# New instruction lists for five engines: the same operations of a gated mix kernel in another written order

## The chip, the core and the metric

The kernel runs on one core of one Trainium2 chip. The metric is the device time of one execution in microseconds (us); a comparison uses the median of several runs. The engines are named as the profile names them: PE is TensorE (PEld its weight loads), DVE is VectorE, ACT is ScalarE, POOL is GpSimd and SP is SyncE, which here issues all data transfers.

## The reference, cut to what matters

```python
L, D, N, F = 2048, 448, 256, 1792           # u: [1, L, D], float32

def _A_ref(u, ...):                          # a long convolution, its kernel made from a diagonal state space
    dt = exp(log_dt); A = -exp(log_A_real) + 1j * A_imag
    C = (C_real + 1j * C_imag) * dt[:, None]
    P = exp((A * dt[:, None])[:, :, None] * arange(L))
    K = 2.0 * einsum("dn,dnl->dl", C, P).real
    y = irfft(rfft(u_t, 2 * L) * rfft(K, 2 * L))[..., :L]
    return y + u * D_skip

def _B_ref(x, w_gate, w_up, w_down):         # a gated linear unit
    return (sigmoid(x @ w_gate) * (x @ w_up)) @ w_down

g = sigmoid((x * gate_w).sum(-1, keepdims=True))
return g * a + (1 - g) * b                   # a, b: the two above, of the same x
```

## The kernel before

The kernel does three kinds of work side by side.

*The linear unit* (tiles of the pools `glu` and `gps`). The rows of x are taken in halves and blocks of 512, the 1792 hidden columns in 14 pieces of 128. `glu_mm` (L1423 to L1428) makes one PSUM tile `gu` of 128x512 from eleven matmuls, in four operations of three or two: values and weights are split into a rounded part (`xs`, `wh`) and a rest (`wl`), so that one product takes several fast matmuls. ACT takes the gate's tanh into `sg` (L1407), DVE multiplies (L1409 or L1412), ACT and DVE split the product into `hh` and `hl`. `glu_down` (L1443 to L1447) multiplies by the down weights `vh`, `vl` into the one PSUM buffer `dn`, with three matmuls, or for some pieces with one plain float32 matmul (L1443), which the profile records as two instructions. DVE adds the result, scaled by one minus the gate, to `ob` (L1462).

*The convolution's kernel* (pools `eg`, `egp`), in 28 chunks of 16 channels. For each, POOL raises powers into `tb`, SP fetches the chunk's phases into `phs`, and `turns` makes angles on PE in two PSUM buffers `tp` (L1232 and L1241), between which ACT rounds (L1236, L1238). ACT then takes sines (L1243, L1244, L1254) into `cs`, DVE multiplies outer products `es` into it (L1261, L1275, L1278), and `contract` (L1290) sums it up on PE, in 32-column quadrants of the array, into `kp`, which ACT copies to `ke` (L1311).

*The transforms* (pools `fu`, `fk`, `fups`, `fkps`), by matmuls with tables: `stage1` (L812) with the table `ft`, of which the pool `fu` holds one buffer of four pieces in turn; a transposition through device memory (`shf`); `spectrum_four` (L845); the product (L889); and the way back (L924). They use row halves, fourths or column halves of the array, and PSUM tiles `fps`.

What sets the order of all this is written out by hand. Each operation has a key: engine, tag of the tile it writes, and a priority number. `PLACE` holds for each key the places of its operations, in the order in which the program makes them, in the list of their engine; each engine, SP with its transfers included, executes its list from front to back. The planner merges the five lists into one sequence and emits it; a tile's buffers are given out in that sequence, and waits follow from who writes and reads each tile.

```python
        for key, places in PLACE.items():
            for o, place in zip(kinds[key], places, strict=True):
                o["place"] = place
        ...
        queue = {e: sorted((o for o in ops if o["eng"] == e), key=lambda o: -o["place"]) for e in engines}
```

Of the kernel before, what the change touches and what calls it, by code (L numbers as in the profile page):

```python
# [28 lines left out]
    ('Act', 'aci', 10): (15, 42,),  # L29
    ('Act', 'aci', 19): (64, 95,),  # L30
    ('Act', 'acr', 10): (14, 40, 53,),
    ('Act', 'acr', 19): (66, 91, 103,),
# [26 lines left out]
    ('Act', 'dots', 1): (28,),  # L59
    ('Act', 'dots', 2): (45,),  # L60
    ('Act', 'dots', 16): (68, 82,),
# [18 lines left out]
    ('Act', 'idn', 10): (13,),  # L80
    ('Act', 'junk', 10): (32, 61,),
    ('Act', 'junk', 19): (78, 81, 143,),
# [12 lines left out]
    ('Act', 'pos_sb', 10): (37, 38,),  # L95
# [25 lines left out]
    ('DVE', 'acr', 19): (152,),  # L121
# [1467 lines left out]
```

## Time and profile before

| | |
|---|---|
| three runs | 687.51, 687.73 and 686.11 us, median 687.51 |
| profiled execution, its own time | 683.66 us |
| its span, first to last instruction | 681.9 us |
| granted TensorE clock, mean | 0.998 |
| PE busy | 669.5 us, 98% of the span, 6568 instructions |
| weight loads (PEld) | 482.7 us, 71% |
| DVE / ACT / POOL busy | 601.7 / 510.3 / 272.4 us (88%, 75%, 40%) |
| data moved | 122.80 MB in 96900 packets, 180 GB/s on the mean |

Matmuls are pipelined in the array and drawn until their results have left it, so that two that follow each other overlap in the profile and the busy time of PE counts time in which nothing new could start; distances between starts tell what a matmul takes. In a line of the waits, the engine, line and tile that waited stand first, then who ended the wait, the total in us, how often, and the longest. In a line of a timeline, the start and the duration in us come first, and in brackets at the end the idle time before the instruction and what ended it. Groups give the total busy time and the mean in ns after the bar, then the idle time before them.

### The profile page before, as it was taken

Reading aid. Unit: us, or ns where it says so; the run is one execution under the profiler, and the core shown is the slowest. Engines: PE = TensorE matmul, PEld = TensorE weight load, DVE = VectorE, ACT = ScalarE, POOL = GpSimd, SP = SyncE. Lnnn points to the kernel's source line nnn. Section 1 sums busy time; section 2 is a strip of 40 time slices with the busy share of each in tenths; the row PEclk is TensorE's granted clock in tenths of the full one; section 3 lists DMA queues with packets and bytes.
Section 4 is the critical chain, followed back from the end, with each engine's and each line's share of the span. In section 5 each row is a group of like instructions: output and inputs, shape, how many; then the busy total and the mean of one; then the engine's idle time right before and its main releaser. Section 6 shows DMA issues by size and latency. Waiting matters only on the chain.

```text
span 681.9 us, 16255 instructions
## 1 busy us (share of the span) xinstructions
PE 669.5 (98%) x6568; PEld 482.7 (71%) x6568; DVE 601.7 (88%) x699; ACT 510.3 (75%) x928; POOL 272.4 (40%) x280
## 2 busy tenths in 40 slices
PE   8999999999999999999999999999999999999996
PEld 7777666877886687676646676788888766556874
DVE  7999999999999999999999999989974389677976
ACT  6688799799999999999999999999842452342110
POOL 0305596554458574494956668534000000000000
PEclk9999999999999999999999999999999999999999
DMA  8969333574893888927977884342969982889855
GB/s 259 247 149 235 100 102 90 132 197 143 225 188 87 178 203 211 262 107 175 183 220 186 180 221 120 123 144 106 208 122 243 278 294 79 269 273 244 148 150 122
DMA packets 96900, 122.80 MB, mean 180 GB/s; under 512 B 31033, under 2 KB 80505, under 8 KB 95801
## 3 DMA queue, kind: packets, MB, share of 16 engines
q1 hardware_dynamic: 96824, 121.76, 69.8%
q8 instruction: 52, 0.85, 0.6%
q14 instruction: 24, 0.19, 0.1%
HBM read 78.16 MB, written 43.58 MB: 179 GB/s over the span
## 4 chain that ended last, share of the span: by engine, by line
PE 73%; ACT 11%; DMA 7%; DVE 5%; issue 2%; SPq 1%; ACTq 0%; DVEq 0%
PE gu_gps L1423 9%; PE gu_gps L1424 8%; PE gu_gps L1425 8%; PE dn_gps L1443 7%; PE kp_egp L1290 6%; PE dn_gps L1445 4%; PE fps_fups L812 4%; PE dn_gps L1446 3%; PE dn_gps L1447 3%; PE tp_egp L1232 3%; PE gu_gps L1427 3%; PE gu_gps L1428 3%; PE tp_egp L1241 3%; DMA us<-fx_fu 3%; DMA ft_fu<-in_s1t_dram 2%; PE fps_fups L889 2%
## 5 line engine op out<-in xcount | busy, mean ns | idle before, releaser
L1423 PE MATMUL gu_gps<-xs_glu,wh_glu 128*128 128x512 f32 x336 | 145.8, 434 | 1.3 <-DVE sg_glu L1412 0.8
L1424 PE MATMUL gu_gps<-xs_glu,wh_glu 128*128 128x512 f32 x336 | 132.0, 393 | 0.0
L1425 PE MATMUL gu_gps<-xs_glu,wl_glu 128*128 128x512 f32 x336 | 131.8, 392 | 0.0
L1278 DVE TENSOR_TENSOR cs_eg<-cs_eg,es_eg 128x2048 f32<-128x2048 f32 x56 | 130.1, 2323 | 1.3
L1222 POOL TENSOR_TENSOR tb_eg<-tb_eg 128x96 f32<-128x96 f32 (+2 forms) x84 | 114.4, 1364 | 6.1
L1261 DVE TENSOR_TENSOR es_eg<-tb_eg 128x1024 f32<-128x1024 f32 x112 | 111.5, 1016 | 2.5
L1423 PEld LDWEIGHTS gu_gps<-xs_glu,wh_glu 128*128 128x128 f32 x336 | 63.3, 189 | 30.3 <-issue 13.5
L1225 POOL TENSOR_TENSOR tb_eg<-tb_eg,bs_eg 128x32 f32<-128x32 f32 x84 | 77.5, 923 | 6.3
L1275 DVE TENSOR_TENSOR cs_eg<-cs_eg,es_eg 128x1024 f32<-128x1024 f32 x56 | 70.5, 1259 | 8.8 <-ACT cs_eg L1254 7.2
L1238 ACT ACTIVATE nn_eg<-cs_eg 128x512 fp32r<-128x512 f32 x112 | 73.1, 653 | 3.8 <-PE tp_egp L1241 2.6
L1424 PEld LDWEIGHTS gu_gps<-xs_glu,wh_glu 128*128 128x128 f32 x336 | 63.3, 188 | 16.4 <-issue 5.6
L1425 PEld LDWEIGHTS gu_gps<-xs_glu,wl_glu 128*128 128x128 f32 x336 | 63.1, 188 | 14.3
L1236 ACT ACTIVATE cs_eg<-tp_egp 128x512 f32<-128x512 f32 x112 | 68.8, 619 | 3.6 <-PE kp_egp L1290 2.2
L1407 ACT ACTIVATE sg_glu<-gu_gps 128x512 f32<-128x512 f32 x56 | 34.1, 609 | 48.8 <-PE gu_gps L1428 47.3
L1243 ACT ACTIVATE cs_eg<-tp_egp 128x512 f32<-128x512 f32 x112 | 67.5, 616 | 2.7 <-PE tp_egp L1241 2.3
L1244 ACT ACTIVATE cs_eg<-tp_egp 128x512 f32<-128x512 f32 x112 | 68.3, 614 | 0.2
L1254 ACT ACTIVATE cs_eg<-cs_eg,half_pi 128x1024 f32<-128x1024 f32 x56 | 66.0, 1179 | 0.1
L1462 DVE SCALAR_TENSOR_TENSOR ob_glu<-dn_gps,og,ob_glu 128x448 f32<-128x448 f32 x70 | 47.4, 677 | 18.4 <-PE dn_gps L1447 17.3
L1290 PEld LDWEIGHTS kp_egp<-cs_eg 128*32 128x32 f32 x3584 | 51.3, 110 | 10.8 <-issue 7.2
L1290 PE MATMUL kp_egp<-cs_eg 128*32 128x64 f32 x3584 | 55.8, 220 | 0.1
L1212 POOL MEMSET tb_eg<- 128x96 f32 x28 | 7.9, 284 | 115.8 <-DVE es_eg L1261 113.6
L1232 PE MATMUL tp_egp<-pos_sb,phs 97*128 97x512 f32 x112 | 50.3, 458 | 1.2 <-ACT cs_eg L1244 1.2
(169 smaller groups left out, 1320.9 us busy)
## 6 DMA issues: line engine op xcount, KB each, us to landing
shf<-fx_fu SPq DMA_DIRECT2D x16, 896.0 KB
fx_fu<-shf SPq DMA_DIRECT2D x16, 896.0 KB
us<-fx_fu SPq DMA_DIRECT2D x16, 896.0 KB
xr_glu<-in_w_dram SPq DMA_DIRECT2D x46, 256.0 KB
uax_fk<-us SPq DMA_DIRECT2D x16, 448.0 KB
ua_fk<-us SPq DMA_DIRECT2D x16, 448.0 KB
xr_glu<-in_w_dram SPq DMA_DIRECT2D x17, 224.0 KB
gt_pre<-in_u_dram SPq DMA_DIRECT2D x8, 448.0 KB
```

Source lines behind the costliest of these rows:

```text
L1222: pool(96 * m, lambda n=n, m=m: G.tensor_mul(g3(n + 1, m), g3(1, m), g3(n, 1).to_broadcast([128, 32, 3, m])))
L1225: pool(32, lambda e=e: G.tensor_mul(t(e + 1), t(e), b(3)))
L1232: op("PE", c_mm(532), lambda: T.matmul(tp.real, phs[:, ph, 128 * nh:128 * nh + 128].bitcast(F32R), pos[:, 512 * i:512 * i + 512], start=Tr ...
L1236: op("Act", c_act(512, True), lambda: S.activation(cs[:, 1, ds, 32:96], block(tp), AF.Copy, bias=MAGIC), [tp], [(cs, ("s", i))], prio)
L1238: op("Act", c_act(512), lambda: S.activation(block(nn), cs[:, 1, ds, 32:96], AF.Copy, scale=-1.0, bias=MAGIC), [(cs, ("s", i))], [nn], prio)
L1261: V.tensor_mul(o.rearrange("p d (i k) -> p d i k", k=ny), x.unsqueeze(3).to_broadcast([128, 16, nx, ny]), y.unsqueeze(2).to_broadcast([128 ...
L1275: op("DVE", c_dve(1024), lambda: V.tensor_mul(cs[:, :, :, 0:32], cs[:, ::-1, :, 63:31:-1], es[:, :, 0:32].unsqueeze(1).to_broadcast([128, ...
L1278: op("DVE", c_dve(2048), lambda: V.tensor_mul(cs[:, :, :, 32:96], cs[:, :, :, 32:96], es[:, :, 32:96].unsqueeze(1).to_broadcast([128, 2, 1 ...
L1290: T.matmul(kp[32 * j:32 * j + 32, q], cs[:, z, 4 * j + q, 64:96], cs[:, z, 4 * j + q, 0:64], start=cs is parts[0] and z == 0 and q == 0, s ...
L1423: T.matmul(p.real, wh[:, k, cs], x[:, k], start=(k == 0), stop=False)
L1424: T.matmul(p.real, wh[:, k, cs], x[:, 4 + k], start=False, stop=False)
L1425: T.matmul(p.real, wl[:, k, cs], x[:, k], start=False, stop=False)
```

## The change

`PLACE` is replaced: for every key the places are numbers found by a new search, "for the best average over three sets of longer durations, fetches and transfers". Nothing else is changed: the same operations with the same operands, sizes and buffers. Of PE's 1043 operations 647 stand at another place, of ACT's 911 578, of DVE's 675 356, of POOL's 276 39 and of SP's 369 transfers 273. The mean distance is 1.43 places on PE, 1.44 on ACT, 1.09 on DVE, 0.24 on POOL and 2.01 on SP, the greatest 12, 23, 24, 8 and 22.

```diff
-    ('Act', 'acr', 10): (14, 40, 53,),
-    ('Act', 'acr', 19): (66, 91, 103,),
+    ('Act', 'acr', 10): (13, 37, 50,),
+    ('Act', 'acr', 19): (63, 91, 103,),
...
-    ('DVE', 'ones', 10): (0,),
+    ('DVE', 'ones', 10): (2,),
...
-    ('DVE', 'rt', 10): (34, 35, 39, 45, 49, 60, 66,),
+    ('DVE', 'rt', 10): (33, 34, 37, 47, 49, 58, 64,),
...
-    ('SP', 'ft', 30): (91, 103, 107, 111, 116, 159, 166, 173,),
+    ('SP', 'ft', 30): (91, 102, 108, 110, 116, 158, 165, 173,),
...
-    ('SP', 'phs', 20): (63, 67, 70, 81, 93, 106, 112, 121, 127, 130, 137, 136, 143, 153, 170, 172, 176, 185, 190, 189,
-        202, 207, 216, 218, 229, 236, 238, 246,),
+    ('SP', 'phs', 20): (60, 67, 74, 80, 103, 107, 112, 121, 125, 130, 137, 136, 148, 163, 167, 174, 175, 184, 189,
+        188, 206, 209, 215, 217, 226, 235, 241, 242,),
...
```

Places of the operations that the prediction speaks of (key, and which of the key's operations, counted from 0). An operation whose own place stays is moved in time by those that now stand before it and no longer do.

| engine | key, number | place before | place after |
|---|---|---|---|
| PE | `fps` 30, 1 and 2 (`stage1`, 141 and 147 us in the profile) | 210, 220 | 212, 220 |
| PE | `gu` 60, 122, 123 and 125 | 214, 218, 211 | 209, 210, 211 |
| PE | `dn` 60, 50 | 208 | 214 |
| PE | `fps` 30, 3 and 4 (155 and 160 us) | 232, 239 | 231, 239 |
| PE | `fps` 30, 19 and 20 (282 and 289 us) | 440, 450 | 440, 451 |
| ACT, PE | `cs` 20, 236 and its reader `tp` 20, 136 (339 us) | 530, 530 | 529, 529 |
| DVE | `ones` 10, 0; `skip` 20, 0; `half_pi` 0, 0 | 0, 1, 25 | 2, 0, 1 |
| DVE, PE | `sg` 5, 2 and the reuse of its PSUM buffer by `gu` 60, 108 (118 us) | 176, 171 | 176, 171 |
| DVE, PE | `rt` 10, 1 and its reader `fps` 10, 0 (17 us) | 35, 14 | 34, 13 |
| SP, PE | `vh` 21, 1 and its reader `dn` 60, 89 (270 us) | 149, 423 | 149, 427 |
| DVE | `ob` 45, 31 (663 us); `ob` 40, 0; `ob` 41, 0 | 650, 649, 646 | 648, 650, 649 |
| DVE, PE | `cs` 20, 79 and its reader `kp` 20, 19 (386 us); `wl` 45, 1 on DVE | 411, 605, 414 | 412, 606, 410 |
| ACT, PE | `cs` 20, 257 and the reuse by `tp` 20, 150 (362 us) | 569, 563 | 569, 563 |
| DVE, PE | `cs` 20, 63 and its reader `kp` 20, 15 (333 us) | 370, 523 | 371, 522 |
| SP | `phs` 20, 13 | 153 | 163 |

More of the change, by code (lines that the diff above doesn't have):

```diff
@@ L28 @@
 PLACE = {
-    ('Act', 'aci', 10): (15, 42,),
-    ('Act', 'aci', 19): (64, 95,),
-    ('Act', 'acr', 10): (14, 40, 53,),
-    ('Act', 'acr', 19): (66, 91, 103,),
[26 rows of a table removed]
-    ('Act', 'dots', 1): (28,),
-    ('Act', 'dots', 2): (45,),
-    ('Act', 'dots', 16): (68, 82,),
[18 rows of a table removed]
-    ('Act', 'idn', 10): (13,),
-    ('Act', 'junk', 10): (32, 61,),
-    ('Act', 'junk', 19): (78, 81, 143,),
[12 rows of a table removed]
-    ('Act', 'pos_sb', 10): (37, 38,),
[13 rows of a table removed]
+    ('Act', 'aci', 10): (15, 40,),
+    ('Act', 'aci', 19): (65, 94,),
+    ('Act', 'acr', 10): (13, 37, 50,),
+    ('Act', 'acr', 19): (63, 91, 103,),
[26 rows of a table added]
+    ('Act', 'dots', 1): (27,),
+    ('Act', 'dots', 2): (47,),
+    ('Act', 'dots', 16): (67, 82,),
[18 rows of a table added]
+    ('Act', 'idn', 10): (12,),
+    ('Act', 'junk', 10): (33, 60,),
+    ('Act', 'junk', 19): (77, 81, 135,),
[12 rows of a table added]
+    ('Act', 'pos_sb', 10): (51, 57,),
[13 rows of a table added]
     ('Act', 'wh', 0): (1, 4,),
     ('Act', 'wh', 1): (6, 7,),
[4 rows of a table removed]
[4 rows of a table added]
     ('Act', 'xs', 0): (0, 2, 3, 5,),
[2 rows of a table removed]
[2 rows of a table added]
     ('DVE', 'aci', 10): (41,),
@@ L120 @@
     ('DVE', 'acr', 10): (89,),
-    ('DVE', 'acr', 19): (152,),
[1 row of a table removed]
+    ('DVE', 'acr', 19): (151,),
[1 row of a table added]
     ('DVE', 'ai', 19): (143,),
[3 rows of a table removed]
[3 rows of a table added]
     ('DVE', 'ci', 19): (140,),
[1 row of a table removed]
[1 row of a table added]
     ('DVE', 'cr', 19): (138, 141,),
[6 rows of a table removed]
[6 rows of a table added]
     ('DVE', 'dt2', 10): (28,),
     ('DVE', 'dtp', 10): (29,),
-    ('DVE', 'dtv', 10): (27,),
[14 rows of a table removed]
-    ('DVE', 'half_pi', 0): (25,),
[24 rows of a table removed]
-    ('DVE', 'ones', 10): (0,),
-    ('DVE', 'p', 10): (16, 17, 19, 21, 22, 23, 26,),
-    ('DVE', 'phs', 20): (2,),
[6 rows of a table removed]
-    ('DVE', 'skip', 20): (1,),
[6 rows of a table removed]
-    ('DVE', 'uax', 40): (536, 539, 546, 547, 561, 558, 571, 572, 575, 579, 584, 585, 591, 590, 596, 595, 622, 623,
[26 rows of a table removed]
+    ('DVE', 'dtv', 10): (26,),
[14 rows of a table added]
+    ('DVE', 'half_pi', 0): (1,),
[24 rows of a table added]
+    ('DVE', 'ones', 10): (2,),
+    ('DVE', 'p', 10): (16, 17, 18, 19, 20, 22, 24,),
+    ('DVE', 'phs', 20): (3,),
[6 rows of a table added]
+    ('DVE', 'skip', 20): (0,),
[6 rows of a table added]
+    ('DVE', 'uax', 40): (536, 538, 545, 546, 556, 561, 571, 569, 575, 578, 583, 582, 591, 590, 595, 596, 622, 623,
[26 rows of a table added]
         1032, 1036, 1040,),
     ('PE', 'fps', -1): (0,),
[6 rows of a table removed]
[6 rows of a table added]
         1039,),
[2 rows of a table removed]
[2 rows of a table added]
         1041,),
[33 rows of a table removed]
[33 rows of a table added]
     ('Pool', 'bsx1', 10): (5, 11,),
     ('Pool', 'bsx1', 19): (17, 49,),
[2 rows of a table removed]
[2 rows of a table added]
         56, 57, 58, 59, 60, 61, 62, 63, 64, 65, 66, 67, 68, 69, 70, 71, 72, 73, 74, 75, 76, 77, 78, 79, 80, 81, 82,
```

510 rows, old and new, of the table PLACE are left out of this document.

## The prediction

> **What bounds the kernel now.** I read the page's first two parts, then the table by windows, then the waits of PE alone, then single gaps in the timeline, and last the grouped lines.
>
> ```profile
> PE 669.5 (98%) x6568; PEld 482.7 (71%) x6568; DVE 601.7 (88%) x699; ACT 510.3 (75%) x928; POOL 272.4 (40%) x280
> ...
> PEclk9999999999999999999999999999999999999999
> ```
> ```profile
> 0.00:50.00 50.00, 48.06 (x195) 36.54 (x196) 43.93 (x102) 34.91 (x61) 6.66 (x11) 1.00 0.84 219
> 50.00:100.00 50.00, 49.42 (x190) 34.56 (x188) 47.52 (x78) 41.90 (x75) 33.47 (x30) 1.00 0.56 150
> 100.00:150.00 50.00, 48.53 (x571) 37.68 (x569) 49.63 (x55) 43.53 (x75) 30.06 (x31) 1.00 0.56 145
> 150.00:200.00 50.00, 49.71 (x602) 39.39 (x591) 48.11 (x45) 48.05 (x89) 26.88 (x30) 1.00 0.70 176
> 200.00:250.00 50.00, 50.00 (x626) 35.87 (x627) 48.56 (x46) 49.84 (x95) 32.73 (x32) 1.00 0.67 148
> 250.00:300.00 50.00, 48.55 (x688) 35.65 (x677) 47.98 (x45) 47.49 (x86) 30.45 (x32) 1.00 0.80 206
> 300.00:350.00 50.00, 48.77 (x667) 32.25 (x666) 48.49 (x47) 48.40 (x88) 36.33 (x37) 1.00 0.79 172
> 350.00:400.00 50.00, 49.93 (x580) 31.98 (x578) 46.63 (x38) 49.76 (x95) 30.25 (x32) 1.00 0.85 213
> ...
> 500.00:550.00 50.00, 50.00 (x379) 39.30 (x378) 22.73 (x34) 18.07 (x34) 0.00 (x0) 1.00 0.88 235
> ...
> 650.00:682.00 32.00, 26.57 (x165) 18.48 (x161) 22.43 (x46) 2.46 (x4) 0.00 (x0) 0.96 0.56 141
> ```
> The columns are length, then busy time of PE, PEld, DVE, ACT and POOL, clock, DMA. PE (TensorE) is busy in 669.5 of 681.9 us, so the end is set by PE's work and by what it loses waiting. Between 100 and 400 us ACT and DVE are nearly full as well (49.84 and 48.56 of 50 in one window), so an operation put too early on PE meets a producer that can't hurry. After 500 us they are under half busy and PE has no idle time. The last 5.4 us are DVE's last additions and the stores. The clock is full until PE has finished.
>
> ```profile
> PE fps_fups L812 <- DMA ft_fu<-in_s1t_dram: 1.8, 4, 0.6
> PE tp_egp L1232 <- ACT cs_eg L1244: 1.2, 1, 1.2
> PE fps_fups L1039 <- DVE ones_pro L1034: 1.1, 1, 1.1
> PE gu_gps L1423 <- DVE sg_glu L1412: 0.8, 1, 0.8
> PE fps_fups L1081 <- DVE rt_pro L1078: 0.6, 1, 0.6
> PE dn_gps L1443 <- DMA vh_glu<-in_w_dram: 0.5, 1, 0.5
> PE tp_egp L1241 <- ACT nn_eg L1238: 0.4, 1, 0.4
> PE gu_gps L1423 <- DVE hh_glu L1409: 0.3, 1, 0.3
> PE dn_gps L1445 <- DVE ob_glu L1462: 0.2, 1, 0.2
> ```
> These twelve waits (total, times, longest) are 6.9 us. That is less than PE loses, since a matmul is drawn longer than its share of the array:
>
> ```profile
> 78.59 0.39 PE L1424 MATMUL gu_gps<-xs_glu,wh_glu 128*128 128x512 f32 x1
> 78.82 0.39 PE L1425 MATMUL gu_gps<-xs_glu,wl_glu 128*128 128x512 f32 x1
> 79.64 0.51 PE L1241 MATMUL tp_egp<-nn_eg,idn 128*128 128x512 f32 x1 [0.44 <-ACT nn_eg L1238]
> 80.13 0.50 PE L1423 MATMUL gu_gps<-xs_glu,wh_glu 128*128 128x512 f32 x1
> 80.46 0.40 PE L1424 MATMUL gu_gps<-xs_glu,wh_glu 128*128 128x512 f32 x1
> ```
> Undisturbed starts are 0.23 us apart (78.59, 78.82). Over the gap it is 0.82, a loss of 0.59 where 0.44 is shown; the next pair but one is 0.33 apart, another 0.10. So a shown gap costs 0.25 more than its figure, and a wait of up to 0.17 (0.40 less 0.23) isn't shown at all. Without the wait at the start, 11 gaps with 5.8 us shown cost 5.8 + 11 x 0.25 = 8.5 us. The hidden ones stretch the first matmul of a group:
>
> ```profile
> L1423 PE MATMUL gu_gps<-xs_glu,wh_glu 128*128 128x512 f32 x336 | 145.8, 434 | 1.3 <-DVE sg_glu L1412 0.8 <-DVE hh_glu L1409 0.3
> L1424 PE MATMUL gu_gps<-xs_glu,wh_glu 128*128 128x512 f32 x336 | 132.0, 393 | 0.0
> L1425 PE MATMUL gu_gps<-xs_glu,wl_glu 128*128 128x512 f32 x336 | 131.8, 392 | 0.0
> ...
> L1241 PE MATMUL tp_egp<-nn_eg,idn 128*128 128x512 f32 x112 | 50.6, 452 | 0.5 <-ACT nn_eg L1238 0.4
> L1232 PE MATMUL tp_egp<-pos_sb,phs 97*128 97x512 f32 x112 | 50.3, 458 | 1.2 <-ACT cs_eg L1244 1.2
> ...
> L1427 PE MATMUL gu_gps<-xs_glu,wh_glu 128*128 128x512 f32 x112 | 46.0, 410 | 0.0
> L1428 PE MATMUL gu_gps<-xs_glu,wl_glu 128*128 128x512 f32 x112 | 43.9, 392 | 0.0
> ```
> ```profile
> 65.73 0.91 PE L1443 MATMUL dn_gps<-vh_glu,hh_glu 128*128 128x448 f32 x2
> 66.14 0.73 PE L1423 MATMUL gu_gps<-xs_glu,wh_glu 128*128 128x512 f32 x1
> 66.71 0.39 PE L1424 MATMUL gu_gps<-xs_glu,wh_glu 128*128 128x512 f32 x1
> ```
> All these do the same 128x512 product. Over 392 or 393 ns, L1423 has 41 x 336 = 13.8 us, L1241 and L1232 (60 + 66) x 112 = 14.1, L1427 18 x 112 = 2.0, together 29.9. Part of it is no wait: behind a plain-f32 matmul (L1443) the next one is charged 0.35 us of that one's time (0.73 against 0.39), and PE's list has 61 such followers, 21.4 us. That leaves 8.5 us hidden, so PE loses about 17 us to waits (2.5%). This is the stock from which the change can take, and to which it can add.
>
> [...]
>
> **The change, part by part.** The five lists hold the same operations, so what could differ by count I counted in both: changes of PE's tile shape (128x128, row halves, column halves, quadrants) 175 before and 175 after; loads of ACT's function table 13 and 13; DMAs 369 and 369. Each is 0 us. What is left are waits. For every operation I took the work that the new list puts ahead of it less the work that it takes away, with the trace's durations. A wait shrinks by the waiting operation's delay less its producer's delay.
>
> The shown gaps, in order of the quoted waits:
> - `ft` (L812), four gaps, around this:
> ```profile
> 142.07 4.90 DMA ft_fu<-in_s1t_dram
> ...
> 275.69 3.33 DMA ft_fu<-in_s1t_dram
> ```
> There is one `ft` buffer, so the load is issued when the second user of the table before has run, and the third waits for it. At 142 us three groups of gate-and-up products (0.68 + 0.45 + 0.80, the last behind a shape change) now stand ahead of that second user and one product of 0.61 comes in behind it: 3.14 us of cover instead of 4.46, a loss of 1.32. At 156 us 0.60 of cover is gained; the gap of 0.35 goes. At 276 us nothing changes; at 284 us 0.57 is gained. Together -0.40 us.
> - `cs` (L1232 at 339): the producer stands 0.66 earlier, the reader 0.78: -0.12.
> - `ones`: two small memsets (0.06 and 0.15) now go first on DVE: -0.21.
> - `sg` (L1423 at 118): the reader is 0.24 later: +0.24.
> - `rt`: DVE makes it 0.86 earlier, PE wants it 0.45 earlier: +0.41.
> - `vh`: the reader is 2.5 us later (four PE operations come first), the load is where it was: gone, 0.5 + 0.25 = +0.75.
> - `nn` at 79.6: +0.09. `hh`: 0. `ob` (L1445): DVE has 0.90 less ahead of it: gone, +0.45.
>
> Sum: **+1.2 us gained**.
>
> The hidden waits. There are 207 links from ACT, DVE or POOL to a PE operation, reuse of a buffer included, whose slack in the trace was under 0.5 us. By the same count the new lists widen them by 0.53 us on average, with a spread of 1.0. A hidden wait is some 0.2 us, so about six in ten disappear: of 8.5 us, **5.3 gained** (bounds 0 and 8.5).
>
> New tight places. 59 PE operations come out earlier than their producers, in 25 stretches; the worst of each add up to 16.4 us, with the dearest at 386 us (1.42, the contraction waiting for DVE, which has a weight split of 0.75 moved ahead), 362 (1.25) and 333 (0.97). 5.1 us lie after 500 us, where ACT has 18.07 and DVE 22.73 of 50 busy and can follow: nothing. Of the other 11.3 the bounds are 0 and 11.3. Nearest are the windows 200 to 250 and 350 to 400, with ACT as full as it gets and PE idle for 0.00 and 0.07 us: tight places mostly vanish there, because PE reaches each one later by what it waited before. I take a third: **3.8 lost**.
>
> SP. One fetch is put clearly later: `phs` for chunk 13, from place 153 to 163.
> ```profile
> 266.62 0.74 SPq L712 DMA_DIRECT2D phs<-phd  x1
> ```
> Its new neighbours were issued near 279, its first reader comes at 286: about 7 us for 96 KB, when the two `ft` loads quoted took 3.33 and 4.90. I price it at 0 (below).
>
> Sum: 1.2 + 5.3 - 3.8 = 2.7 us. The profiled execution took 683.66 (span 681.9), 3.85 under the median of the three runs; it would come to 681.0, and the median from 687.51 to **684.8**.
>
> **Rivals.**
> - *No change* (0.34): the tight places take 4.4 to 8.6 us instead of 3.8, or fewer hidden waits go; around 687.2. For it: every operation moved only one or two places on average. Against: the links with under 1 us widened in every class I counted.
> - *Slower* (0.21): the chunk pipeline between 320 and 390 us. There contractions and phase products were put ahead while ACT and DVE have no reserve (48.40 and 48.49 of 50). At full price the time is 687.5 + 11.3 - 6.5 = 692.3; it turns slower once over 8.6 us are paid.
> - *A late `phs`* (0.02): if it takes twice the longer of those loads (9.8 us), PE and ACT stop together for about 3 us at 286: 684.8 + 3 = 687.8, and over 689.6 from 12 us on.
> - *Much faster* (0.12, within faster): all hidden waits go and the tight places cost nothing: 687.5 - 1.2 - 8.5 = 677.8.
> - *The clock* (0.01): no gap in the trace is over 1.2 us, and the only window below 1.00 is the one in which PE has stopped for 5.4. [...]
>
> **How the numbers follow.** Within 0.3% (2.1 us, about what a measurement here can tell from no change) is 685.4 to 689.6. Faster 0.42 holds the forecast and the much faster case; same 0.34; slower 0.24 holds the chunk pipeline, the fetch and the clock. The ends are 677.8 and 692.3; I leave one in ten out on each side: 679.0 to 691.0. The forecast's own range is 682 to 687.
>
> **What would show it.** Right: the wait on `vh` and that of L1445 on `ob` gone; the `ft` wait at 147 us up to about 2 us shown and the one at 159 gone; the mean of L1423 down from 434 to under 425; shown idle time of PE before 500 us down from 7.0 to about 6. Wrong: new entries in PE's waits on `cs` between 330 and 390 us, ACT or DVE idle there with PE waiting, a wait for `phs` near 286, or PE idle after 500 us.

## The result, and the profile after

| | before | after |
|---|---|---|
| median (lowest to highest), 22 executions each | 687.12 us (683.61 to 691.55) | 683.02 us (681.93 to 689.33) |
| profiled execution, its own time | 683.66 us, span 681.9 | 682.07 us, span 680.3 |
| PE busy | 669.5 us | 668.7 us |

The ratio of the new kernel's time to the old one's is 0.9944, with a 95% interval of 0.993 to 0.9958: faster by 4.1 us at the median, where 684.8 us (2.7 less) had been forecast. One thing in the table needs an explanation from the start: the two profiled executions are only 1.6 us apart. The old kernel's profiled execution was one of its quickest (the lowest of the 22 is 683.61); the new kernel's stands 0.95 us under its own median.

The page after, part 1 and the clock row of part 2:

```profile
PE 668.7 (98%) x6568; PEld 480.6 (71%) x6568; DVE 598.5 (88%) x699; ACT 508.8 (75%) x928; POOL 272.7 (40%) x280
...
PEclk9999999999999999999999999999999999999999
```

The same work, the same durations. The waits of PE after (total, times, longest):

```profile
PE fps_fups L1039 <- DVE ones_pro L1034: 1.2, 1, 1.2
PE tp_egp L1232 <- ACT cs_eg L1244: 0.7, 2, 0.5
PE tp_egp L1232 <- DMA phs<-phd: 0.6, 1, 0.6
PE gu_gps L1423 <- DVE sg_glu L1412: 0.5, 1, 0.5
PE gu_gps L1423 <- DVE hh_glu L1409: 0.5, 2, 0.2
PE gu_gps L1423 <- DVE hl_glu L1409: 0.4, 1, 0.4
PE fps_fups L812 <- DMA ft_fu<-in_s1t_dram: 0.3, 1, 0.3
PE gu_gps L1423 <- ACT xs_glu L1350: 0.3, 1, 0.3
PE gu_gps L1424 <- DVE xs_glu L1354: 0.2, 1, 0.2
PE tp_egp L1241 <- ACT nn_eg L1238: 0.2, 1, 0.2
PE fps_fups L1081 <- DVE rt_pro L1078: 0.2, 1, 0.2
PE gu_gps L1424 <- DVE xs_glu L1356: 0.2, 1, 0.2
PE dn_gps L1445 <- DVE ob_glu L1462: 0.2, 1, 0.2
```

Against the list of before: `ft` went from 1.8 us in four waits to 0.3 in one, `rt` from 0.6 to 0.2, `sg` from 0.8 to 0.5, `cs` from one of 1.2 to two of 0.7 together, and `vh` is gone. New are `phs`, `hl` and `xs`. And the groups in which hidden waits would show (total busy, mean ns):

```profile
L1423 PE MATMUL gu_gps<-xs_glu,wh_glu 128*128 128x512 f32 x336 | 144.2, 429 | 1.6 <-DVE sg_glu L1412 0.5 <-DVE hh_glu L1409 0.5 <-DVE hl_glu L1409 0.4
...
L1241 PE MATMUL tp_egp<-nn_eg,idn 128*128 128x512 f32 x112 | 50.7, 453 | 0.3 <-ACT nn_eg L1238 0.2
L1232 PE MATMUL tp_egp<-pos_sb,phs 97*128 97x512 f32 x112 | 50.3, 457 | 1.3 <-ACT cs_eg L1244 0.7 <-DMA phs<-phd 0.6
```

L1423 fell by 5 ns a matmul, the other two stand where they were. So one profile against the other shows 1.6 us, in small waits. The other 2.5 us of the gain must then be in executions that the first profile of before doesn't show, and the experiments went after those.

### The profile page after: what moved, and what is told of

It reads as the page before. It is cut to its first block, busy times and chain, and to the rows that moved or that the text cites. A ratio compares the mean times of both kernels' runs of the same rounds, so it can differ in the third digit from the quotient of the medians.

```text
span 680.3 us, 16240 instructions
## 1 busy us (share of the span) xinstructions
PE 668.7 (98%) x6568; PEld 480.6 (71%) x6568; DVE 598.5 (88%) x699; ACT 508.8 (75%) x928; POOL 272.7 (40%) x280
## 4 chain that ended last, share of the span: by engine, by line
PE 84%; DVE 8%; ACT 3%; DMA 2%; issue 2%; SPq 0%; ACTq 0%; DVEq 0%
PE gu_gps L1423 10%; PE gu_gps L1424 10%; PE gu_gps L1425 10%; PE kp_egp L1290 7%; PE dn_gps L1443 7%; PE dn_gps L1445 5%; PE tp_egp L1232 4%; PE dn_gps L1446 4%; PE dn_gps L1447 4%; PE tp_egp L1241 4%; PE gu_gps L1427 3%; PE gu_gps L1428 3%; PE fps_fups L812 3%; PE fps_fups L845 3%; PE fps_fups L889 2%; PE fps_fkps L889 2%
## 5 line engine op out<-in xcount | busy, mean ns | idle before, releaser
L1423 PE MATMUL gu_gps<-xs_glu,wh_glu 128*128 128x512 f32 x336 | 144.2, 429 | 1.6 <-DVE sg_glu L1412 0.5
L1222 POOL TENSOR_TENSOR tb_eg<-tb_eg 128x192 f32<-128x192 f32 (+2 forms) x84 | 116.4, 1386 | 6.0
L1261 DVE TENSOR_TENSOR es_eg<-tb_eg 128x1024 f32<-128x1024 f32 x112 | 110.1, 1006 | 3.4 <-POOL tb_eg L1225 1.0
L1423 PEld LDWEIGHTS gu_gps<-xs_glu,wh_glu 128*128 128x128 f32 x336 | 63.2, 188 | 30.5 <-issue 14.1
L1236 ACT ACTIVATE cs_eg<-tp_egp 128x512 f32<-128x512 f32 x112 | 69.5, 631 | 4.3 <-PE tp_egp L1232 2.9
L1244 ACT ACTIVATE cs_eg<-tp_egp 128x512 f32<-128x512 f32 x112 | 69.7, 629 | 0.4 <-PE tp_egp L1241 0.3
L1243 ACT ACTIVATE cs_eg<-tp_egp 128x512 f32<-128x512 f32 x112 | 68.8, 631 | 1.3 <-PE tp_egp L1241 1.1
L1225 POOL TENSOR_TENSOR tb_eg<-tb_eg,bs_eg 128x32 f32<-128x32 f32 x84 | 67.1, 799 | 5.9
L1414 ACT ACTIVATE hh_glu<-sg_glu 128x512 fp32r<-128x512 f32 x34 | 22.3, 656 | 39.5 <-DVE sg_glu L1412 23.2
```

The costliest lines, as they stand in the source:

```text
L1222: pool(96 * m, lambda n=n, m=m: G.tensor_mul(g3(n + 1, m), g3(1, m), g3(n, 1).to_broadcast([128, 32, 3, m])))
L1236: op("Act", c_act(512, True), lambda: S.activation(cs[:, 1, ds, 32:96], block(tp), AF.Copy, bias=MAGIC), [tp], [(cs, ("s", i))], prio)
L1243: op("Act", c_act(512, True), lambda: S.activation(cs[:, 0, ds, 32:96], block(tp), AF.Abs), [tp], [(cs, ("c", i))], prio)
L1244: op("Act", c_act(512, True), lambda: S.activation(cs[:, 1, ds, 32:96], block(tp), AF.Sin, scale=TWO_PI), [tp], [(cs, ("s", i))], prio, ta ...
L1261: V.tensor_mul(o.rearrange("p d (i k) -> p d i k", k=ny), x.unsqueeze(3).to_broadcast([128, 16, nx, ny]), y.unsqueeze(2).to_broadcast([128 ...
L1423: T.matmul(p.real, wh[:, k, cs], x[:, k], start=(k == 0), stop=False)
```

## The experiments

All ratios are to the old kernel, run on the same chip alongside. "Segment" kernels take the new places in one stretch of time and the old ones in the rest; they were cut where all engines' lists hold the same operations up to that point.

### Which stretch carries the gain

```diff
-PLACE = old
+PLACE = new               # all_new: the changed kernel once more
+PLACE = new | old         # first240: new up to 240 us, old behind
+PLACE = old | new | old   # mid240_300: new from 240 to 300 us
+PLACE = old | new         # last300: new from 300 us
```

> All five new lists, the changed kernel itself, as the yardstick for the three parts beside it. Every theory: ratio 0.994 to the kernel before, some 3.9 us less; a profile with PE some 1.5 to 2.5 us ahead at its last matmul.

> New places on all engines up to 240 us of the profile, the old ones behind (the cut lies where each engine's old and new list have done the same operations). Theory F, the gain is at the waits for fetched data (a table at 147 and 160 us, weights and tables between 265 and 290): 0.9 to 1.1 us less, ratio 0.9985. Rival W, the gain is in many short hidden waits behind ACT and DVE all along, by the share of the time in which they are full: 1.5 us less or more.

> New places only between 240 and 300 us. Theory F: 1.3 to 2.2 us less in the profile, the wait for the down weights near 269 and for the tables at 279 and 288 gone, and the largest part of the gain of the median, ratio 0.996 to 0.997. Rival W: 0.5 us less, as a ninth of the time.

> New places only after 300 us. Theory F: no change within 0.5 us, ratio 0.9993 to 1.0007, since PE waits for hardly any fetch there. Rival W: 1.5 to 2 us less, since the stretch from 300 to 450 us holds the most links that were widened. A second rival, the end: 0.8 us more, since in the profile of the changed kernel the lead of 2.4 us at the last matmul is 1.6 at the end of the span.

| kernel | median us | ratio | 95% interval |
|---|---|---|---|
| all_new | 683.33 | 0.9925 | 0.9902 to 0.9948 |
| first240 | 684.08 | 0.9933 | 0.9907 to 0.9959 |
| mid240_300 | 686.10 | 0.9971 | 0.995 to 0.9993 |
| last300 | 689.40 | 1.0026 | 0.9999 to 1.0054 |

(6, 6, 12 and 12 executions.) The gain sits before 300 us; the new lists behind it bring nothing. Neither theory had foreseen this pattern: F gave first240 about 1 us, where its ratio stands for 4.6, and W gave last300 1.5 to 2 us, where it gained none. The profile that pointed to a reason came by chance: the profiled execution of first240 took 686.52 us, 2.4 over its median and the longest of its six. Its waits of PE:

```profile
PE kp_egp L1290 <- issue: 3.1, 1, 3.1
```

"issue" means that PE waited for no semaphore and no data that the profile shows. PE's timeline there (start, duration, in brackets the idle time before):

```profile
248.54 1.55 PE L1290 MATMUL kp_egp<-cs_eg 128*32 128x64 f32 x96
253.21 1.08 PE L1290 MATMUL kp_egp<-cs_eg 128*32 128x64 f32 x32 [3.12 <-issue]
254.22 0.80 PE L1232 MATMUL tp_egp<-pos_sb,phs 97*128 97x512 f32 x1
254.82 0.63 PE L1423 MATMUL gu_gps<-xs_glu,wh_glu 128*128 128x512 f32 x1
255.25 0.63 PE L1424 MATMUL gu_gps<-xs_glu,wh_glu 128*128 128x512 f32 x1
...
257.34 0.39 PE L1423 MATMUL gu_gps<-xs_glu,wh_glu 128*128 128x512 f32 x1
257.57 0.39 PE L1424 MATMUL gu_gps<-xs_glu,wh_glu 128*128 128x512 f32 x1
```

A contraction of 128 matmuls on data that is all there breaks off after 96 and goes on 3.12 us later, and then the products stand 0.43 us apart instead of 0.23: half clock. With a granted clock of 0.81 and 0.85 in the two windows below that makes 3.4 us of it ((0.19 + 0.15) x 5 / 0.5). The windows of first240 around it, and below them one of all_new (length, busy PE, PEld, DVE, ACT, POOL, clock, DMA share, GB/s):

```profile
250.00:255.00 5.00, 1.88 (x42) 1.52 (x34) 3.33 (x5) 0.92 (x1) 2.55 (x4) 0.81 0.97 220
255.00:260.00 5.00, 5.00 (x21) 4.05 (x20) 2.68 (x2) 4.22 (x8) 0.00 (x0) 0.85 0.69 168
```
```profile
250.00:255.00 5.00, 5.00 (x143) 4.21 (x142) 4.99 (x7) 4.49 (x9) 3.77 (x5) 1.00 0.88 226
```

The other engines lose time there as well. The reading that the rest of this document tests is that PE had waited for its next instructions. The profile lists loads of instructions as a queue of their own (row of before; after has the same 52 and 0.85 MB):

```profile
q8 instruction: 52, 0.85, 0.6%
```

Each of the 52 is recorded with 16384 bytes, and PE has 13308 instructions, weight loads included, 255.9 for each load; so they are taken to be PE's, one for each 256. In before and after each record begins with PE between 101 instructions ahead of a multiple of 256 and 159 behind it. By estimate from such records a load is taken here to be due when PE has got to within 66 instructions of the multiple. Over the fourteen profiles of this document the records of the loads lie 0.9 us behind that point at the median, half of them between 0.1 us ahead and 2.6 us behind. How far PE got beyond that point before its stops is counted below. The 17th is due at PE's instruction 4286 (counted from 0 in the order of starts), near 241 us. In first240 its record stands at 250.92, 10 us late; PE's last matmul ahead of the stop had ended at 250.1. What lies in that time is a burst that SP issues just before (rows of before, first240 and after; us<-fx_fu are four transfers of 896 KB):

```profile
241.17 5.62 SPq L712 DMA_DIRECT2D us<-fx_fu  x4
```
```profile
239.73 5.62 SPq L712 DMA_DIRECT2D us<-fx_fu  x4
```
```profile
240.48 5.48 SPq L712 DMA_DIRECT2D us<-fx_fu  x3
252.49 0.34 SPq L712 DMA_DIRECT2D bs_eg<-bsd  x1
252.87 1.47 SPq L712 DMA_DIRECT2D us<-fx_fu  x1
```

The theory formed here, called Theory I in what follows, is that the old kernel usually loses some 4 to 5 us near 250 us because this load is asked for just behind the burst and waits for it, and the new lists move the two against each other so that the load gets through. The old kernel's first profile would then be one of the executions in which the load slipped in front. Its rival: the loss is in the waits for tables and tiles that the profiles name. last300, which is the old order up to 300 us, had the stop too:

```profile
PE kp_egp L1290 <- issue: 3.0, 1, 3.0
```

### The old order profiled again, and parts of the new one near 240 us

```diff
+# before_copy: the old kernel unchanged
-            for _ in range(WAKE):              # before_plus64: WAKE is 14, the warm-up of PE
+            for _ in range(13):
                 T.matmul(wake[:, :128], ones.real, ones.real, start=True, stop=True)
+            for i in range(17):
+                j = i % 4
+                T.matmul(wake[32 * j:32 * j + 32, 0:2], ones[:, 0:32], ones[:, 0:2], start=True, stop=True)
+# us_late: on SP the transfer us0, 4 moved behind the fetch bs, 6; all else old
+# compute_mid: mid240_300 with the old list on SP
```

> The kernel before once more, for another profiled execution. Theory I (an instruction fetch of PE, late behind a burst of copies of the spectrum near 241 us, stops PE in most executions of the kernel before, and did not in the one first profiled): if this execution takes 686 to 688 us, its profile has PE without work for about 3 us near 252 us, in the middle of one contraction, put down to no releaser, with the clock down behind it, and the fetch of instructions that belongs there comes some 10 us late; if it takes under 685, it has not. Rival N (the first profile was low by noise that lies everywhere): the extra time is spread over the span.

> The lists of before; the 14 warming matmuls at the start are 13, and 17 small ones in 32-column quadrants come behind them, so that PE executes 64 instructions more before the first product and reaches every bound of 256 instructions 64 earlier. In the first profile the fetch in question is asked for near instruction 4280, at 242 us; 64 earlier is 238, ahead of the burst. Theory I: 3 to 4 us less, ratio 0.9945 to 0.9965, although no operation that matters is changed. Rival N, or a gain from the order alone: no change, ratio 1.000 within 0.001.

> The lists of before, but one transfer in SP's list moved: the last of the four copies of the spectrum in the burst (896 KB) goes behind the next fetch of the chunk's tables, as in the new list, so that the burst is three copies and the fourth follows some 10 us later. Theory I: the late fetch of instructions lands 2 to 3 us sooner and PE no longer runs dry: 3 to 4 us less, ratio 0.9945 to 0.9965. Rival W (the gain is in the order of PE, ACT and DVE): no change, ratio 1.000 within 0.001.

> Between 240 and 300 us the new places on PE, ACT, DVE and POOL, SP's list as before. Theory F (waits for fetched data): 1 us less, since the wait for the down weights near 269 goes with the reader's place on PE. Theory I alone: nothing, the burst is as before, ratio 0.999 to 1.001. Rival W: as much as the same stretch with SP's list, ratio 0.997.

| kernel | median us | ratio | 95% interval |
|---|---|---|---|
| before_copy | 693.0 (one execution) | | |
| before_plus64 | 692.41 | 1.0088 | 1.0056 to 1.012 |
| us_late | 687.31 | 1.0006 | 0.998 to 1.0033 |
| compute_mid | 686.29 | 0.9992 | 0.9964 to 1.0019 |

At 693.0 us the second profiled execution of the old kernel is longer than all 28 others that ran alongside (682.55 to 691.21, median 686.80) and outside both cases of its expectation, so it can show the stop but not how common it is. It has the stop, and longer waits for `ft` than the first (3.7 us against 1.8):

```profile
PE fps_fups L812 <- DMA ft_fu<-in_s1t_dram: 3.7, 3, 1.8
PE kp_egp L1290 <- issue: 3.5, 1, 3.5
```

By starts of the same PE instructions, it falls behind the first profile by 2.5 us between 135 and 150 us (the `ft` waits) and by 5.3 us between 241 and 261 us (the stop with the half clock behind it). In no other stretch does it lose or win more than 0.8 us. The `ft` wait of 1.8 us, too, had half clock behind it; the last section has the rows.

us_late was meant to relieve the load by taking one of the four transfers away. It missed: the stop was still there, 2.1 us, and the median stayed, so in this execution three transfers ahead of the load were enough. (The profiled execution, 684.87 us, is the quickest of its twelve, so that the others may lose more.) compute_mid, for which Theory I alone forecast no gain, had none that can be measured, but its interval also holds what the two other theories gave it; that its profile has no stop, the theory had not said.

before_plus64 missed in sign. It put 64 more instructions where PE has nothing else to do, so that each load falls 64 instructions earlier in the work. The stop near 250 us went, but others came:

```profile
PE kp_egp L1293 <- issue: 2.9, 3, 1.7
PE gu_gps L1431 <- issue: 1.9, 1, 1.9
```

(Lines stand 3 further down in this kernel.) Together they are 4.8 us, and the granted clock of this execution was half from 152.53 to 155.95 and from 343.68 to 350.51 us, which by estimate costs another 5 (half of 10.2). The median is 5.6 us above the old kernel's.

The times of the 17th load in twelve profiles, read from the load queue's records, beside the burst's first issue and PE's instruction 4286 (us; "ahead" is the third column less the second):

```
kernel          burst issued (n)  PE instr. 4286  ahead   load's record   stop
before_copy       244.22 (4)        245.70        1.48      255.64         3.5
last300           242.75 (4)        244.24        1.49      253.85         3.0
us_late           240.98 (3)        242.47        1.49      251.13         2.1
before            241.17 (4)        242.68        1.51      242.46         none
compute_mid       241.07 (4)        242.35        1.28      243.90         none
first240          239.73 (4)        240.93        1.20      250.92         3.1
mid240_300        242.44 (3)        243.64        1.20      243.83         none
all_new           241.19 (3)        241.77        0.58      240.56         none
after             240.48 (3)        241.06        0.58      240.46         none
first300          241.01 (3)        241.58        0.57      241.03         none
before_noburst     none             243.20                  242.25         none
after_noburst      none             243.16                  242.15         none
```

With the old order the burst is issued 1.5 us ahead of that instruction: three of four profiles stop. With the new lists on one side of 240 us it is 1.2 to 1.3: one of three. With the new lists on both sides it is 0.6: none of three. The load is recorded either within 1.6 us of the instruction or 8.7 to 10 us behind it, with nothing between, as if it either slipped in front of something or waited behind it. These are single executions, and the kernels differ in the size of the burst too. `first300` and the last two rows come from the next group, which tests the cause itself.

Two more readings of the same records bear on Theory I. First, the next load, the 18th, is due at instruction 4542, some 10 us behind the burst, and its delay goes with the burst in every profile: 0.7 and 0.8 us without it, 2.0 to 3.6 us behind three transfers (six profiles), 7.3 to 9.2 us behind four (six profiles). In before it was due at 251.05 and recorded at 260.22; PE did not stop for it; it reached the instruction 259 further on only at 264.06, 3.8 us after the record. Second, the stops stand at one place of the count, as they would if a block of 256 instructions were lacking. The six profiles with stops in the contractions or the products have fourteen, and each time PE stood before the instruction 193 behind a multiple of 256 and went on 2.2 to 3.3 us after the record of the load that was due 259 instructions earlier. (A few waits of 0.2 to 0.7 us put down to issue in the transforms after 540 us stand elsewhere and are not explained.)

### The burst taken away, and the new order with its loads shifted

```diff
-            for q in range(2):                        # spectrum_u
+            for q in range(1 if h == 0 else 2):       # before_noburst, after_noburst
-  lambda b=b, c=c: us[:, c, b]                        # product
+  lambda b=b, c=c: us[:, c, b % n]                    # n = 4 if h == 0 else 8
+# first300: new places up to 300 us, old behind
+# after_plus64: the new kernel with the 64 instructions of before_plus64
```

> The old lists without the four transfers of 896 KB (us, second half of the columns' first half) that SP issues at 241 us; the product reads the first half twice instead, so part of the computation is left out. Theory I (the old order's typical execution stops PE near 250 us, because a load of 256 instructions waits behind these four): no idle time of PE put down to issue over 0.5 us between 240 and 260 us, the load there lands within 3 us, and the median is 3.5 to 5 us below before, ratio 0.993 to 0.995. Theory II (the old order loses its time at its waits for tables and tiles, whatever is transferred at 241 us): less than 1.5 us, ratio 0.998 to 1.0.

> The new lists without the same four transfers; part of the computation is left out, as in the kernel with the old lists. Theory I: the new order already avoided the stop in most of its executions, so that less comes off than with the old lists, 0 to 1.5 us against the new order with the transfers; the new order then stands 1.5 to 2.5 us below the old without them (the part of the gain that comes from waits). Theory II: the new order stands 3.5 to 4.5 us below the old without the transfers too, as with them.

> The new lists with 30 more small matmuls (64 instructions) in the warm-up at the start, where PE has nothing else: every later load of 256 instructions is asked for 64 instructions earlier in the order, nothing else changes. Theory I (where the loads fall against the large transfers decides over some 4 us, and the search did not know of it): stops of 1.5 to 3.5 us put down to issue appear in the profile, and the ratio to before is 0.998 to 1.005; if the loads happen to miss the transfers again, 0.994 to 0.996. Theory II (the new order is better by its waits alone): 0.994 to 0.996 in either case, and no stop.

> The new lists on all five engines until 300 us, the old ones behind. Theory I (the gain is made before 300 us; behind it the new order is worth nothing or costs a little): ratio to before 0.990 to 0.995, 680.5 to 684 us, at or below the kernel with all new lists, and no stop of PE for its instructions in the profile. Theory II (the gain is spread over the whole, and the old lists behind 300 us meet tiles that come at other times than theirs): 0.995 to 1.0.

| kernel | median us (lowest to highest) | ratio | 95% interval |
|---|---|---|---|
| before_noburst | 683.88 (682.38 to 685.90) | 0.9954 | 0.9931 to 0.9977 |
| after_noburst | 684.72 (681.94 to 687.23) | 0.9975 | 0.995 to 1.0 |
| after_plus64 | 689.89 (686.00 to 692.63) | 1.0035 | 1.0009 to 1.0061 |
| first300 | 682.28 (681.10 to 685.93) | 0.9927 | 0.9906 to 0.9949 |

Without the four transfers the median of the old order falls by 3.3 us, and its highest time to 685.90, from 691.4 for the old kernel alongside. The gain is a little under the 3.5 expected at least; the interval, 1.6 to 4.7 us, leaves out the rival's 1.5, if narrowly. PE's only wait between 230 and 300 us there is

```profile
PE fps_fups L812 <- DMA ft_fu<-in_s1t_dram: 0.3, 1, 0.3
```

and no stop; the load was recorded at 242.25, ahead of its instruction. Of its twelve executions eleven have a mean granted clock of 0.998 or more, against 14 of the old kernel's 34 alongside, so the half clock went with the burst. This is the direct test, and Theory I stands. One thing the test doesn't part: the burst may also keep other fetches waiting. The first profile of before has 1.5 us of waits for `ft` and `vh` between 265 and 290 us, and only 0.3 are left here, so up to about 1.2 us of the 3.3 may be theirs.

The test went further than I had expected in one point: without the burst the new order is not measurably faster than the old (684.72 and 683.88), where I had expected 1.5 to 2.5 us for its shorter waits. By the two intervals a lead of the new order of up to some 0.9 us is not excluded (an estimate). So most of the gain, 3.3 of 4.1 us, is had by the old order alone once these transfers are away. Why the new order without the transfers is above the new order with them, by 1.7 us of medians from different groups of runs, I can't say: its profile has 0.9 us of a wait for `fx` that neither after nor all_new has, and SP's list runs earlier without the transfers, but nothing tested that.

after_plus64 shows that the gain belongs to this order with this count of instructions. With 64 instructions more in the warm-up (the products behind it start within 0.1 us of where they did by 12.5 us), the new order is slower than the old kernel, within the ratio that Theory I gave. The profiled execution, 692.63 us, is the slowest of its twelve. Its waits of PE:

```profile
PE kp_egp L1293 <- issue: 4.6, 4, 1.6
...
PE gu_gps L1428 <- issue: 1.0, 1, 1.0
```

These are 5.6 us of stops of 0.6 to 1.6 us, shorter ones than the 1.5 to 3.5 expected, where by the two ratios the kernel lies 0.0091 of 687 or 6.3 us above the new kernel. One of them:

```profile
348.48 1.86 PE L1293 MATMUL kp_egp<-cs_eg 128*32 128x64 f32 x115
351.93 0.42 PE L1293 MATMUL kp_egp<-cs_eg 128*32 128x64 f32 x13 [1.59 <-issue]
...
352.61 0.40 PE L1426 MATMUL gu_gps<-xs_glu,wh_glu 128*128 128x512 f32 x1
352.84 0.40 PE L1427 MATMUL gu_gps<-xs_glu,wh_glu 128*128 128x512 f32 x1
```

This one came without a burst: ahead of it SP had issued 160 KB at 342.02 us and 896 KB at 342.41, and nothing more until 352.80. A contraction's 128 matmuls and 128 weight loads, the 256 instructions of one load, start within 1.78 us (before and after), and in this kernel PE went on 2.2 to 3.3 us after the record of the load that it lacked (349.2 in this case, 351.93 to go on). By these figures, as an estimate, a load recorded when a contraction has begun comes too late for the end of it. In before, after and the two kernels with 64 more instructions, eleven unbroken runs of more than 227 instructions of a contraction begin 9 to 29 instructions behind such a point. Eight of them are long enough to reach the 259th instruction behind it, and all eight break off there, with 0.3 to 1.9 us between two starts that are else 0.04 apart. All eight are in the shifted kernels. The three others, one of them in after, end before that instruction and ran through; before has none.

first300 is as fast as the new kernel and no faster within the interval; ten of its eleven executions lie at 681.10 to 683.06, one at 685.93. Its profile has no stop. No kernel was found that beats the new one measurably.

One more number for Theory I comes from the old kernel's 34 executions alongside this group: the 14 with a mean granted clock of 0.998 or more have a median of 684.6 us, the 20 with 0.997 or less one of 687.8. In the two other groups the difference is smaller, 2.2 us (3 and 20 executions) and 2.4 us (11 and 17). Half clock for 3.4 us, as behind the stops of 3.0 us and more, takes about 0.0025 off the mean clock, so this is what executions with and without such a stop would look like. It is no proof of the stop: before_copy had half clock behind an `ft` wait as well, and us_late's stop left the clock at 1.00.

## Why the prediction was right in the number and wrong in the reason

- *The time.* 684.8 with a range of 679 to 691 was forecast, 683.0 came, faster as thought likeliest. The forecast's own sum was 2.7 us; profile against profile it was 1.6, median against median 4.1.
- *From the profiled execution to the median.* This step failed. The prediction noted that before's profiled execution was 3.85 us under the median and carried the distance over unchanged. Over 22 executions each the distance is 3.46 us before and 0.95 after, and these 2.5 us are more than half of the 4.1 gained. The runs put most of the distance down to the stop for instructions, with its half clock, that this execution happened not to have: taking the burst away took 3.3 us off the old order's median. How much of it is late `ft` loads instead is open.
- *Shown gaps, +1.2.* Too small. PE's idle time before 500 us went from 7.0 to 5.4 us (about 6 forecast), but 1.9 of the 5.4 are gaps that before did not have. The old gaps alone shrank by about 3.5 us. `vh` is gone, `rt` and `sg` shrank by 0.4 each (0.41 and 0.24 forecast), `ones` grew by 0.1 (0.21). Three parts failed: the `ft` wait at 147 us was to grow by 1.32 and is not there, the `cs` wait at 339 was to grow by 0.12 and fell from 1.2 to 0.46, and the wait of L1445 for `ob` was to go and stayed at 0.2 (last row of the waits above). The `ft` gap at 159 us, for which 0.35 was put, is 0.28 in the trace.
- *Hidden waits, +5.3.* Much too large. L1423 fell from 434 to 429 ns (under 425 forecast), 336 times 5 ns or 1.7 us, but L1427 rose from 410 to 422, 112 times 12 ns or 1.3 us back:

```profile
L1427 PE MATMUL gu_gps<-xs_glu,wh_glu 128*128 128x512 f32 x112 | 47.3, 422 | 0.0
```

  That is 0.4 us net, by these rounded means. The count of links with little slack took every link's widening as time that PE gets back; the rows show that hardly any of it came back, and why was not tested for single links.
- *New tight places, -3.8.* Too large as well. Of the entries for `cs` between 330 and 390 us that would have shown them, one came, of 0.23 at 330.5; after 500 us PE has the one wait of 0.2 that it had before. What came new is this and the five rows `phs`, `hl` and `xs` above, 1.9 us.
- *The sum.* That 2.7 came near the 1.6 between the profiled executions is luck: by these rows the three terms are about 3.5, 0.4 and -1.9, together 2.0, where 1.2, 5.3 and -3.8 were forecast, and the errors nearly cancel. That the median came within 2 us of the forecast is luck too, since its larger part lies outside the sum.
- *`phs` of chunk 13, 0.* Right: no wait near 286 us. The wait for `phs` that did come is another chunk's, at 243 us.
- *The clock, 0.01.* The rival was called nearly impossible because no gap in the profile was over 1.2 us. Two further profiles of the old order, before_copy and last300, have one of 3.5 and 3.0 us with half clock behind it; I had judged all executions by one. In before_copy 1.77 us of idle time within 3.41 us, too, had half clock behind them (last section).
- *The other rivals.* Neither the chunk pipeline nor a late `phs` at 286 us showed; the gain beyond the forecast's did not come from hidden waits either.

What neither the prediction nor its rivals had is the supply of instructions. The row `q8 instruction` with 0.6% of the transfers' time stood on the page of before and looked too small to matter.

Left open: the `ft` waits vary between profiles of the old order from 0.5 us (us_late, before_noburst) through 1.8 (before) to 3.7 (before_copy), and with the new order before 240 us from none (all_new) to 1.0 (first240). How much of the gain at the median is theirs was not measured apart; with the burst gone, hardly any difference between the orders is left that could hold it. That the burst makes the load late is shown by taking it away; in which queue the load waits is not.

## What to carry to other kernels

When a median lies well above a profiled execution of the same kernel, profile again before costing a change: what the slow executions lose may be the larger part, and it may be in a wait that the first profile lacks. Look for waits of PE put down to "issue" in the midst of a group of equal matmuls whose data is there, and hold their times against the instruction loads and against large transfers issued just before; keep a burst of large transfers from being issued just ahead of a load (here three or four transfers of 896 KB, issued 1.2 to 1.5 us ahead, went with a load 8.7 to 10 us late in four of seven profiles, and it took more than moving one of four transfers), and small dense matmuls from beginning just as one is due (here 256 instructions in 1.78 us). An order that came out of a search can owe its gain to such a coincidence: adding instructions that cost nothing themselves is a cheap test of it, and here it turned 4.1 us of gain into 2.4 us of loss (by the ratio).

## What the runs showed of the hardware

- The queue of instruction loads has 52 records of 16384 bytes in before and in after, 255.9 of PE's 13308 instructions for each. Fourteen stops of PE, in six profiles, stand at the 259th instruction behind the point at which a load is taken to be due, and PE went on 2.2 to 3.3 us after the record of that load. With the waits put down to issue after 540 us, which stand elsewhere, the profiles show such idle times of 0.2 to 3.5 us. A load due 1.2 to 1.5 us behind the issue of three or four transfers of 896 KB was recorded within 1.6 us (three profiles) or 8.7 to 10 us late (four); the next one, due some 10 us behind, was recorded 2.0 to 3.6 us late behind three and 7.3 to 9.2 us late behind four.
- The granted clock changed at multiples of 3.41 us. In before and in after it was full for 672.43 us, 197 times 3.4133, and half from there on, from 679.7 and 677.7 us, where PE's last matmuls end at 676.7 and 674.3. In all fourteen profiles it falls to half only at a whole number of these windows behind the point at which it first became full (before_copy: 42 and 74 windows; first240: 72), and until PE has finished, half clock lasted one window, once two (6.83 us, before_plus64). In these profiles it went with the idle time of PE within one window, not with the length of a gap:

```profile
145.54:148.95 3.41, 1.64 (x9) 1.06 (x9) 3.31 (x3) 2.40 (x6) 3.30 (x2) 1.00 1.03 326
148.95:152.36 3.41, 3.41 (x84) 2.87 (x85) 2.55 (x5) 2.09 (x4) 2.63 (x5) 0.50 0.24 97
```
```profile
249.10:252.51 3.41, 2.12 (x101) 1.65 (x99) 3.31 (x5) 2.81 (x5) 3.25 (x4) 1.00 1.03 255
252.51:255.93 3.42, 2.60 (x39) 2.10 (x40) 1.37 (x2) 1.46 (x3) 1.70 (x3) 1.00 0.40 105
```

  The first two rows are of before_copy: the `ft` wait left PE busy for 1.64 us, 1.77 idle, and the next window had half clock. The others are of us_late: the longer stop of 2.11 us fell across two windows, 1.30 and 0.82 idle, and the clock stayed full. Up to PE's last matmuls, half clock came behind the windows with 1.67 us idle or more (1.67, 1.77, 2.01, 2.98, 3.03 and 3.17) and behind no full-clock window with 1.65 us or less; the second of the two in a row came behind a window, itself at half clock, with 0.95.
